# A fused delta-rule attention and maxout FFN kernel: loads asked for in another order, and two blocks written from another queue

## The chip, the cores and the metric

The kernel runs on one core of a Trainium2 chip. A core has TensorE (PE), VectorE (DVE), ScalarE (ACT), GpSimd (POOL) and SyncE (SP), each with its own in-order stream of instructions, and 16 DMA engines[...]. The metric is the device time of one execution in microseconds (us), lower is better; the median of three runs before the change is 530.83 us (530.11 to 531.15).

## The reference

Two stages follow each other. The first is a delta-rule recurrence for 4 batches x 8 heads, 768 steps and head size 48; the second a maxout FFN over the 3072 tokens of width 384.

```python
k_n = k / (norm(k) + 1e-06)
for t in range(S):
    y[:, :, t] = q_t @ state
    v_old = state^T k_t
    state = state + beta_t * outer(k_t, v_t - v_old)
x = y.transpose(0, 2, 1, 3).reshape(B * S, H * D)      # 3072 x 384
h = maximum(maximum(x @ w1, x @ w2), x @ w3)           # 384 -> 768
out = h @ w_out                                        # 768 -> 384
```

## The kernel before, in words

The recurrence is done in 12 chunks (c) of 64 steps. A chunk has two units, n = 2c and 2c + 1, each of two batches with all heads; four units make a group m of two chunks, so there are 6 groups, and group m's tokens are the 512 that FFN stage m takes. For a unit, `turn` (L361, L367) transposes the keys (part 0) and queries (part 1) on PE and copies them to SBUF; `gram` (L438) multiplies keys with keys (`at`, copied at L455) and keys with queries (`pt`, copied at L449 or masked at L422). Within a chunk a triangular system has to be solved. Its 32-wide blocks are gathered as one system per partition: the `at` blocks of a group go to DRAM (`to_dram`, L468, four DMAs a unit), `blocks` reads them back as `x_bl` (L515), and `solve` eliminates on DVE (L551, then pairs of L565 and L569). The result y goes to DRAM (`y_d`, L591) and comes back as `ut` (L600, eight DMAs). Group 0, the opening, does it without DRAM: `to_blocks`, a transpose, the elimination in halves of 16, a transpose back (L573), copies into `ut` (L584 on ACT, L586 on DVE or GpSimd). Then the parts are joined: `halves_z` (p_e, L674) and `halves_u` (p_f, L691; negated copies L681 on DVE, L683 on ACT) for the halves of 16; `join_z` (p_z, L709; copies L712, L714) and `join_u` (p_j, L723; L681, L683) for those of 32. `new` (p_u, L768), `step` (p_s), `to_y` (p_y) and `to_x` (p_x) carry the recurrence and lay the result out as the FFN's input `xt`.

The FFN's weights come as 24 pieces of 384 KB: `fetch` (L215) loads one into `w_bits` (five buffers, oldest first), and one step of `conv` (the generator `weights`) converts one on ACT (L238, L239, L240, into `mant` and `up`, two buffers each) and then joins the piece before it: a shift on DVE (L250) and an add on GpSimd (L254). Pieces 0 to 17 are w1, w2 and w3, 18 to 23 are w_out.

Every engine executes in the order in which the program is written (a manual schedule), so the text is the schedule. After the opening, the loop over `ffn(0)` has 31 steps i, 18 of a half-width p_h (L926), 9 of a full-width one, then the output layer (p_o, L958). In each step the tables name what else is put in: `fetch` and `conv` by i, `FIRST` and `EARLY_LINKS` by letters (t = turn, g = gram, z and j = joins, u = new, s = step, S = a step of `solve`). In EARLY_LINKS the units of g0 to g3 are 8 to 11, at steps 12, 14, 16 and 17. Steps of `solve(1)` lie in steps 0 to 13; its write to DRAM falls in step 12, the reads in step 13. `blocks(2)` reads at step 18. In step 18 `some(conv, 1)` stands ahead of d0 d1 z0 z1, and in step 19 it stands ahead of j0.

Two buffers matter in the opening: unit n's queries lie in place n mod 3 of `qall`, so unit 3's load waits until unit 0's have been turned; and `wo_sb` lends its room to the squares of the keys and to the second system, which is cleared there (L1022) before `solve(1)` starts.

The lines around the first edit (before):

```python
first_blocks()
some(solving, 1)
nc.gpsimd.memset(in_wo(1), 0.0)
load_beta()
load_q(2, (nc.gpsimd, nc.gpsimd))
```

Of the kernel before, what the change touches and what calls it, by code (L numbers as in the profile page):

```python
# [23 lines left out]
def kernel(  # L24
# [31 lines left out]
    nc = tc.nc  # L56
# [50 lines left out]
    one_queue = (nc.sync, nc.sync)  # L107
# [19 lines left out]
    def place(n):  # L127
        return n % NK if n < 12 else n % 4
# [4 lines left out]
    def load_q(n, queues=one_queue):  # L133
        load(q, qpad[n % NQ], n, queues)
# [14 lines left out]
    def load_beta():  # L149
        for i in range(4):  # L150
            cc, half = divmod(i, 2)
            nc.gpsimd.dma_start(
                out=beta_bl[32 * i : 32 * (i + 1)],
                in_=beta.rearrange(
                    "b h (m c f i) -> c f (b h) m i", c=2, f=2, i=BL
                )[cc, half],
            )
# [53 lines left out]
    def fetch(queue=nc.scalar):  # L211
        if fetched[0] < len(pieces):
            _, src, (a, b) = pieces[fetched[0]]
            st = work.tile([128, 2 * 384], U32, name="w_bits", bufs=5)
            queue.dma_start(  # L215
                out=st.rearrange("p (a b) -> p a b", a=a), in_=src
            )
            staged.append(st)
            fetched[0] += 1
# [50 lines left out]
    def small(name, *shape):  # L270
        one = name[-1] == "0" or name[-2:] == "bl" or name == "warm"
        return work.tile([128, *shape], FP32, name=name, bufs=2 - one)
# [60 lines left out]
    def first_norms():  # L333
        norm(nrm_0, ksum_0, small("root0", 2, 2, H), small("newton0", 2, 2, H))
# [10 lines left out]
    def turn(n, parts=(0, 1), copy=nc.scalar.copy):  # L345

        if n not in kqts:
            if n == 6:
                kqts[n] = work.tile([128, KT, TOK], FP32, name="xt").rearrange(
                    "p k t -> p (k t)"  # L350
                )[:, 0 : NP * 4 * C].rearrange(
                    "p (j b i t) -> p j b i t", b=2, i=2, t=C
                )
            else:
                kqts[n] = work.tile([128, NP, 2, 2, C], FP32, name="kqt", bufs=6)
        kqt = kqts[n]
        p_t = ps_two("p_t")
        for i in parts:
            src = (kpad[place(n)], qpad[n % NQ])[i]
            for j in range(NP):  # L360
                nc.tensor.transpose(  # L361
                    p_t[:, i, j * 128 : (j + 1) * 128],
                    src[:, 2 * j : 2 * j + 2],
                    ident,
                )
        some = slice(parts[0], parts[-1] + 1)
        copy(  # L367
            kqt.rearrange("p j b i t -> p i (j b) t")[:, some],
            p_t.rearrange("p i (x t) -> p i x t", t=C)[:, some],
        )  # L370
# [56 lines left out]
    def gram(n, parts=(0, 1), queues=one_queue, copy=nc.scalar.copy, later=False):  # L427
        kqt, g = kqts[n], n % 2
        p_g = ps_two("p_g")

        whole = len(parts) == 2 and not g
        for j in range(NP):
            for par in range(2):
                for bb in range(2):
                    kq = kqt[dims(par), j, bb ^ g]
                    for i in (0,) if whole else parts:
                        c0 = j * 128 + i * C
                        nc.tensor.matmul(  # L438
                            p_g[
                                rows(bb ^ (g * i)), par, c0 : c0 + C * (1 + whole)  # L440
                            ],
                            kq[:, 0],
                            kq if whole else kq[:, i],
                        )
        p_v = p_g.rearrange("p two (j i t) -> p two j i t", j=NP, i=2)
        if 1 in parts:
            pt = pts[n] = square("pt")
            if later:
                copy(by_par(pt), p_v[:, :, :, 1])  # L449
            else:  # L450
                masked(pt, p_v[:, :, :, 1])
        if 0 not in parts:
            return
        at = ats[n] = square("at")
        copy(by_par(at), p_v[:, :, :, 0])  # L455
        if queues:
            to_dram(n, queues)
# [23 lines left out]
    def in_wo(i):  # L481
        n = BL * BL + BL
        return wo_sb.rearrange("p t d -> p (t d)")[:, n * i : n * (i + 1)].rearrange(
            "p (s r) -> p s r", s=2
        )
# [15 lines left out]
    def first_blocks():  # L501
        xs[0] = work.tile([128, 2, HB * BL + HB], FP32, name="x_bl", bufs=1)
        nc.vector.transpose(
            out=in_rows(xs[0]), in_=in_rows(in_wo(0)).rearrange("p x i -> p i x")
        )
# [159 lines left out]
    def halves_z(c):  # L665
        if c > 1:
            halves_t(c)
        at = [ats[2 * c + g] for g in range(2)]
        second = ut[c % NU].rearrange("p g h (f two x) -> p g h f two x", two=2, x=HB)
        for hs, p_v, copy in heads_of(c, "p_e", BL):  # L670
            for i, h in enumerate(hs):
                for bb, g in TILES:
                    r = rows(bb)
                    nc.tensor.matmul(  # L674
                        p_v[rows(bb ^ g), g, i], at[g][r, h], second[r, g, h, :, 1]
                    )
            copy(zs[c % NU][:, :, span(hs)], p_v)
# [294 lines left out]
    def some(gen, n):  # L972
        for _ in range(n):
            if next(gen, gen) is gen:
                break
# [15 lines left out]
    def keys(n, queues=one_queue, copy=nc.scalar.copy):  # L991
        gram(n, (0,), queues, copy)
# [25 lines left out]
    to_blocks(2, (nc.scalar, nc.gpsimd, nc.scalar, nc.gpsimd))  # L1018
    to_blocks(3, (nc.vector, nc.scalar, nc.vector, nc.scalar))
    first_blocks()  # L1020
    some(solving, 1)
    nc.gpsimd.memset(in_wo(1), 0.0)  # L1022
    load_beta()
    load_q(2, (nc.gpsimd, nc.gpsimd))
    p_n = flipped(kflip_0)
    nc.scalar.copy(ksum_0[:, :, 1], p_n.rearrange("p (c h) -> p c h", c=2))
    turn(4, (0,))
# [3 lines left out]
    turn(6, (0,))  # L1031
    turn(0, (1,))
    load_q(3, (nc.gpsimd, nc.gpsimd))
    keys(6)
    gram(0, (1,), None, later=True)
    turn(7, (0,))
# [4 lines left out]
        fetch(nc.sync)  # L1041
    blocks(1)
    load_v(1)
    for n in (2, 3):
        turn(n, (1,))
    for n in (2, 3):
        gram(n, (1,), None, later=True)
    some(solving, HB + 1)
    halves_t(0)
    halves_z(0)  # L1050
    first_norms()
    for c in range(2):
        scale(c, nrm_0[:, c])
# [52 lines left out]
        e=halves_z, f=halves_u, d=turn_t1,  # L1106
    )
    MADE = dict(V=load_v, P=prep_values)
    UNIT = dict(t=turn, g=gram, K=load_k, L=lambda n: load_blocks(n, nc.sync))
    OF_KEYS = dict(S=lambda n: some(solving, n), T=lambda n: turn(n, (1,)), P=lambda n: gram(n, (1,)))  # L1110

    def links(m, names):
        for name in names.split():
# [3 lines left out]
            elif f in MADE and m + 1 < GROUPS:  # L1117
                MADE[f](2 * (m + 1) + i)
            elif f in UNIT and m + 1 < GROUPS:
                UNIT[f](4 * (m + 1) + i)  # L1120
            elif f == "N" and m + 2 < GROUPS:
# [12 lines left out]


    CONVERTED = {*range(6), *range(11, 25)}
    for i, _ in enumerate(ffn(0)):
        if i - 1 in CONVERTED:
            fetch(nc.sync if i < 10 else nc.gpsimd)
        if i in (18, 19, 25):  # L1140
            some(conv, 1)
        if i == 20:
            solving = solve(2)
            some(solving, 1)
        if i == 21:
            some(solving, 3)
        queries(FIRST.get(i, ""))
        links(1, EARLY_LINKS.get(i, ""))
        if i in CONVERTED and i not in (18, 19):
            some(conv, 1)  # L1150
        if 3 < i < 14:
            some(solving, (2, 1, 2, 2, 3, 3, 3, 3, 2, 2)[i - 4])
        if i in (5, 7):
            prep_values(i // 2)
        if i in (1, 7):
            for n in range(2):
                load_k(8 + 2 * (i > 1) + n, (nc.gpsimd, nc.gpsimd))
        if i == 0:
            load_v(3)
        if i in (0, 2):  # L1160
            load_q(5 + i // 2)
        if i == 11:
            load_q(11, (nc.gpsimd, nc.gpsimd))
        if i in (10, 21):
            load_v(4 + i // 21)
        if i == 18:
            blocks(2)
        if i == 23:
            prep_values(4)
        if i > 21:  # L1170
            some(solving, (3, 2, 3, 2, 2, 5, 5, 5, 4)[i - 22])
        if i in (27, 28, 29):
            load_blocks(i - 15, nc.sync)
        if i in (15, 17, 19, 22, 25, 27):
            less_first((15, 17, 19, 22, 25, 27).index(i))
        if 27 <= i < 30:
            turn_first((2 * (i - 27), 2 * (i - 27) + 1))


    RECURS.update(x=y_blocks, w=read_y, X=turn_y, p=prep_values)  # L1180
    UNIT.update(t=turn_blocks, K=lambda n: load_k(n, (nc.gpsimd, nc.gpsimd)))
    MADE.update(V=lambda c: load_v(c, nc.gpsimd))
# [43 lines left out]
```

## Time and profile before

| | before |
|---|---|
| time, median of 3 | 530.83 us |
| profiled span | 528.4 us |
| PE busy | 499.5 us, 95% of the span |
| DVE, ACT, POOL busy | 309.2, 164.7, 186.1 us |
| chain that ended last, by engine | PE 77%, DVE 11%, DMA 4%, SP queue 4% |
| PE waiting for the queries (p_t from qall) | 3.3 us, once |
| PE waiting for ut from y_d (p_z) | 3.0 us, twice |

A busy time is summed over one engine's instructions. The chain is followed back from the last instruction to what released each; its shares say where the time went, while a busy share only says how full an engine was. The first 118 us are where PE isn't full.

### The profile page before, as it was taken

The numbers are of one execution on the slowest core, as the hardware profiler recorded it, in microseconds if no ns is written. First come the engines' busy times: TensorE is split into PE (matmuls) and PEld (weight loads), VectorE is DVE, ScalarE is ACT, GpSimd is POOL, SyncE is SP. The second block draws the span as 40 slices with busy tenths as digits, with TensorE's granted clock in tenths as the row PEclk, the third lists the DMA queues.
The fourth block names the chain that finished last, engine by engine and source line by source line (L and its number), as shares of the span: only waits on it lengthen the run. The fifth ranks groups of instructions, "written<-read, shape, count | busy, mean of one in ns | idle before, by whom it ended". The sixth has DMA issues, their size and how long they took to land.

```text
span 528.4 us, 18036 instructions
## 1 busy us (share of the span) xinstructions
PE 499.5 (95%) x7840; PEld 308.4 (58%) x7840; DVE 309.2 (59%) x695; ACT 164.7 (31%) x302; POOL 186.1 (35%) x306
## 2 busy tenths in 40 slices
PE   6567899979999999999999999999999999999996
PEld 5456677855556555566555565555565555654453
DVE  5855999866997351499662899654887231111100
ACT  5556573685422152120142201242101411011000
POOL 7504255553365471962095880501230000000000
PEclk9855789998999999999999999999999999999999
DMA  8972948494116771654494553734334202130011
GB/s 113 214 157 79 179 124 150 105 261 114 33 37 165 150 145 31 141 131 103 104 165 92 145 138 95 162 54 89 88 85 107 43 2 62 52 68 0 0 27 34
DMA packets 110591, 53.47 MB, mean 101 GB/s; under 512 B 93808, under 2 KB 104976, under 8 KB 110512
## 3 DMA queue, kind: packets, MB, share of 16 engines
q1 hardware_dynamic: 100016, 34.70, 31.4%
q0 software_dynamic: 8384, 17.22, 13.7%
q8 instruction: 62, 1.02, 0.8%
q10 hardware_dynamic: 2112, 0.39, 0.5%
q14 instruction: 17, 0.14, 0.1%
HBM read 39.17 MB, written 13.11 MB: 99 GB/s over the span
## 4 chain that ended last, share of the span: by engine, by line
PE 77%; DVE 11%; DMA 4%; SPq 4%; issue 2%; ACT 1%; POOL 1%; DVEq 0%; ACTq 0%; POOLq 0%
PE p_h L926 33%; PE p_o L958 25%; PE p_g L438 3%; DVE wo_sb L569 3%; PE p_u L768 2%; PE p_m L906 2%; PE p_y L810 2%; SPq L120 2%; DVE tmp L565 2%; PE p_k L740 2%; DMA qall<-in_q_dram 2%; PE p_s L791 1%; PE p_q L740 1%; PE p_j L723 1%; DMA ut<-y_d 1%
## 5 line engine op out<-in xcount | busy, mean ns | idle before, releaser
L926 PE MATMUL p_h<-xt,w_sb 128*128 128x512 f32 (+1 forms) x522 | 221.4, 569 | 2.7 <-DVE h L940 1.3
L926 PEld LDWEIGHTS p_h<-xt,w_sb 128*128 128x128 f32 x522 | 96.8, 194 | 88.8 <-issue 80.5
L958 PE MATMUL p_o<-wo_sb,h 128*128 128x384 f32 x288 | 97.8, 489 | 0.0
L940 DVE TENSOR_TENSOR h<-h,p_h 128x512 f32<-128x512 f32 (+1 forms) x48 | 29.7, 619 | 95.2 <-PE p_h L926 95.1
L958 PEld LDWEIGHTS p_o<-wo_sb,h 128*128 128x128 f32 x288 | 53.7, 190 | 35.7 <-issue 0.5
L565 DVE TENSOR_TENSOR tmp<-x_bl,y_bl 128x31 f32<-128x31 f32 (+20 forms) x139 | 54.0, 388 | 4.1
L964 ACT COPY o_sb<-p_o 128x384 f32<-128x384 f32 x24 | 11.5, 480 | 134.1 <-PE p_o L958 128.1
L569 DVE TENSOR_TENSOR y_bl<-y_bl,tmp 128x31 f32<-128x31 f32 (+20 forms) x139 | 48.5, 349 | 4.8
L936 ACT ACTIVATE h<-p_h 128x512 f32<-128x512 f32 x30 | 17.9, 597 | 87.9 <-PE p_h L926 86.5
L958 PE MATMUL p_o<-w_sb,xt 128*128 128x384 f32 x120 | 42.0, 486 | 0.0
L396 POOL DMA_DIRECT2D turned<-in_q_dram x72 | 39.3, 553 | 5.2 <-POOL turned L391 2.5
L438 PE MATMUL p_g<-kqt 48*64 48x64 f32 (+1 forms) x1216 | 27.5, 240 | 6.0 <-DVE nt_bl L263 3.7
L254 POOL TENSOR_TENSOR w_sb<-mant,up 128x384 int32<-128x384 int32 x18 | 18.6, 1036 | 41.1 <-DVE mant L250 23.5
L438 PEld LDWEIGHTS p_g<-kqt 48*64 48x64 f32 x1216 | 24.2, 141 | 14.4 <-ACT kqt L367 7.3
L958 PEld LDWEIGHTS p_o<-w_sb,xt 128*128 128x128 f32 x120 | 22.8, 190 | 15.9
L120 POOL DMA_DIRECT2D kpad<-in_k_dram x32 | 21.9, 691 | 14.3 <-PE p_s L791 14.3
L287 POOL TENSOR_TENSOR v_t<-v_t,nrm 128x768 f32<-128x768 f32 x12 | 18.2, 1520 | 23.4 <-DVE nrm L266 14.4
L798 DVE TENSOR_TENSOR st<-st,p_s 48x768 f32<-48x768 f32 (+1 forms) x18 | 17.1, 949 | 15.0 <-PE p_s L791 14.8
L422 DVE TENSOR_TENSOR pt<-p_g,mask 128x512 f32<-128x512 f32 x20 | 13.7, 689 | 17.2 <-PE p_g L438 17.2
L139 POOL DMA_DIRECT2D v_t<-in_v_dram x12 | 9.9, 832 | 34.2 <-PE p_u L768 33.3
L391 POOL MEMSET turned<- 128x96 f32 x18 | 3.3, 191 | 50.0 <-DVE kqt L412 50.0
L768 PEld LDWEIGHTS p_u<-v_t,ut 64*64 64x64 f32 x768 | 13.5, 141 | 8.7 <-issue 7.8
(152 smaller groups left out, 618.6 us busy)
## 6 DMA issues: line engine op xcount, KB each, us to landing
w_bits<-in_moe_w_dram SPq DMA_DIRECT2D x14, 384.0 KB, 3.5
out_dram<-o_sb SPq DMA_DIRECT2D x48, 96.0 KB, 2.2
turned<-in_q_dram POOLq DMA_DIRECT2D x72, 48.0 KB, 2.8
kpad<-in_k_dram POOLq DMA_DIRECT2D x32, 96.0 KB, 4.3
y_x<-y SPq DMA_DIRECT2D x16, 192.0 KB
qall<-y_x SPq DMA_DIRECT2D x32, 96.0 KB, 2.7
at_d<-at SPq DMA_DIRECT2D x80, 32.0 KB, 2.4
ut<-y_d SPq DMA_DIRECT2D x40, 64.0 KB, 3.1
```

The source lines that it names most:

```text
L120: queues[bb].dma_start(out=dst[rows(bb ^ g), :, 0:D], in_=src[2 * bb + g, :, c * C : (c + 1) * C, :].rearrange("h p d -> p h d"),)
L254: nc.gpsimd.tensor_tensor(out=dst.bitcast(I32), in0=mant_v.bitcast(I32), in1=up_v, op=ALU.add)
L287: nc.gpsimd.tensor_tensor(out=vts[c], in0=vts[c], in1=nrm[:, :, :, None].to_broadcast([128, 2, H, D]), op=ALU.mult,)
L396: (queue, nc.gpsimd)[i].dma_start(out=t[p0 : p0 + 32, bb, at : at + NP * 2 * D].rearrange("p (j x) -> p j x", j=NP), in_=(k, q)[i][2 * bb ...
L438: nc.tensor.matmul(p_g[rows(bb ^ (g * i)), par, c0 : c0 + C * (1 + whole)], kq[:, 0], kq if whole else kq[:, i],)
L565: nc.vector.tensor_tensor(out=t_v, in0=row.to_broadcast(t_v.shape), in1=column.to_broadcast(t_v.shape), op=ALU.mult,)
L569: nc.vector.tensor_tensor(out=rest, in0=rest, in1=t_v, op=ALU.subtract)
L768: nc.tensor.matmul(p_v[rows(bb ^ g), g, i], ut[c % NU][rows(bb), g, h], rhs[rows(bb), g, h],)
L926: nc.tensor.matmul(p_h, w_sb[i][:, t, f * 128 : (f + 1) * 128], xt[:, t, lo : lo + w], start=(t == 0), stop=(t == KT - 1),)
L936: nc.scalar.activation(out=h, in_=p_h, func=mybir.ActivationFunctionType.Relu)
L940: nc.vector.tensor_tensor(out=h, in0=h, in1=p_h, op=ALU.max)
L958: nc.tensor.matmul(p_o, stays, moves, start=(n == 0), stop=(n == len(terms) - 1))
```

## The change

Three things are changed, all in the order of instructions or in the queue that issues a transfer; the arithmetic stays as it is.

1. In the opening, the load of unit 2's queries is issued by GpSimd ahead of its share of the solve; the clear of the second system and the beta loads go behind the load of unit 3's queries. Unit 2's Gram with its queries follows its turn at once, and unit 3's is put behind `halves_z(0)`, so that the copies into `ut` don't stand behind it.
2. The weight loads of steps 12 to 21 are laid out anew: one in step 8, none in steps 15 to 17, in which the substitution's result is on its way to DRAM and back, and two each in steps 18 and 19. The conversion of step 19 moves behind that step's links.
3. The `at` blocks of units 10 and 11 are written to DRAM through GpSimd's queue instead of SP's.

```diff
     first_blocks()
+    load_q(2, (nc.gpsimd, nc.gpsimd))
     some(solving, 1)
-    nc.gpsimd.memset(in_wo(1), 0.0)
-    load_beta()
-    load_q(2, (nc.gpsimd, nc.gpsimd))
...
     load_q(3, (nc.gpsimd, nc.gpsimd))
+    nc.gpsimd.memset(in_wo(1), 0.0)
+    load_beta()
...
-    for n in (2, 3):
-        turn(n, (1,))
-    for n in (2, 3):
-        gram(n, (1,), None, later=True)
+    turn(2, (1,))
+    gram(2, (1,), None, later=True)
+    turn(3, (1,))
     some(solving, HB + 1)
     halves_t(0)
     halves_z(0)
+    gram(3, (1,), None, later=True)
     first_norms()
...
-    UNIT = dict(t=turn, g=gram, K=load_k, L=lambda n: load_blocks(n, nc.sync))
+    UNIT = dict(
+        t=turn, K=load_k, L=lambda n: load_blocks(n, nc.sync),
+        g=lambda n: gram(n, queues=(nc.gpsimd,) * 2 if n in (10, 11) else one_queue),
+    )
...
     CONVERTED = {*range(6), *range(11, 25)}
+    FETCHED = {8: 1, 12: 1, 13: 1, 14: 1, 18: 2, 19: 2, 20: 1, 21: 1}
     for i, _ in enumerate(ffn(0)):
-        if i - 1 in CONVERTED:
-            fetch(nc.sync if i < 10 else nc.gpsimd)
-        if i in (18, 19, 25):
+        if 0 < i < 7:
+            fetch(nc.sync)
+        for _ in range(FETCHED.get(i, 0)):
+            fetch(nc.gpsimd)
+        if i in (18, 25):
             some(conv, 1)
...
-        if i in CONVERTED and i not in (18, 19):
+        if i in CONVERTED and i != 18:
             some(conv, 1)
```

## The prediction

> **What bounds the kernel now.** I read the page's slices first. PE is full from about the tenth slice on (one slice is 13.2 us); what can be won lies ahead of that and in the dip of the granted clock in the tenth digit.
>
> ```profile
> PE   6567899979999999999999999999999999999996
> PEclk9855789998999999999999999999999999999999
> ```
>
> Then the chain that ended last, in order of time (start us, us, what). It shows the two places that the change touches.
>
> ```profile
> 22.19 5.67 DMA qall<-in_q_dram
> 28.00 2.03 PE p_t L361 x8
> 30.02 1.97 PE p_g L438 x63
> ...
> 32.02 0.59 ACT pt L449
> ...
> 32.62 1.05 ACT ut L584
> ...
> 102.95 6.06 DMA y_d<-wo_sb
> ...
> 112.07 4.78 DMA ut<-y_d
> ...
> 116.98 0.96 PE p_z L709 x51
> 117.93 4.47 PE p_h L926 x6
> ```
>
> First place: the queries of units 2 and 3 arrive at 27.9, PE turns them, makes two Grams, ACT copies them out, and only then does ACT copy the solved block (ut, L584). DVE's timeline shows that the block had been ready earlier, and who waited for ACT:
>
> ```profile
> 27.10 1.92 DVE L573 STREAM_TRANSPOSE x_bl<-y_bl 128x1024 f32<-128x1024 f32 x1
> 34.78 0.71 DVE L646 STREAM_TRANSPOSE t<-ut 128x512 f32<-128x512 f32 x1 [4.49 <-ACT ut L584]
> ```
>
> The transpose ends at 29.02; ACT starts at 32.62: 3.6 us lost on the chain. From 54 to 100 us the chain is DVE's (the elimination L565/L569 and what is put between), with hardly a wait, so an earlier start there is kept.
>
> Second place: the result of the substitution goes to DRAM (6.06 us for the second 256 KB) and comes back; PE stands at p_z for 0.39 and 2.65 us, and the next p_h takes 4.47 us where its neighbours take 2.77, because the clock fell: 119.5 to 122.9 us at half. GpSimd's timeline shows what ran on the DMA engines and on GpSimd then (brackets: idle before, and releaser):
>
> ```profile
> 101.43 0.75 POOL L215 DMA_DIRECT2D w_bits<-in_moe_w_dram  x1
> 102.20 1.01 POOL L254 TENSOR_TENSOR w_sb<-mant,up 128x384 int32<-128x384 int32 x1
> 103.15 0.77 POOL L215 DMA_DIRECT2D w_bits<-in_moe_w_dram  x1
> ...
> 105.32 0.75 POOL L215 DMA_DIRECT2D w_bits<-in_moe_w_dram  x1
> ...
> 107.34 0.57 POOL L215 DMA_DIRECT2D w_bits<-in_moe_w_out_dram  x1
> 108.87 1.00 POOL L254 TENSOR_TENSOR w_sb<-mant,up 128x384 int32<-128x384 int32 x1 [0.96 <-ACT up L240]
> ```
>
> After 123 us PE has no long idle left, so what is won before it should stay to the end.
>
> **What the skill says.** "TensorE: Matmul & The Clock Gate", What's actually happening: the array runs at half clock after an idle window of about 3.4 us and comes back after a busy one. The trace agrees: one 3.4 us stretch at half after the p_z waits. "DMA: Bandwidth & Descriptors", Queues, rings and completion order: each DMA engine takes turns between the queues that have work. The trace agrees: between 105 and 110 us the DMA share is 0.97, and the y_d write takes 6.06 us where the same 256 KB take 4.1 at the median of the later stages. "SBUF — State Buffer", Who interferes with whom: GpSimd's writing of descriptors can be held up while DVE has the shared ports. Here GpSimd's ten issues at L215 lie between 0.55 and 0.78 us beside a busy DVE, so I do not expect it to matter.
>
> **The change part by part.**
>
> *Queries sooner.* Unit 2's load now goes out when GpSimd is free of the block copies, at 12.5 instead of 21.5; the clear of y_bl behind it ends near 15 and is needed by L542 at 17.72: hidden. Unit 3's load needs PE's turn of unit 0's queries (ends 19.0), so it goes out near 19.1 instead of 22.9. With the 4 to 5.7 us to landing of these loads both are there by 18 and by 25. The clear of wo_sb and the beta loads move behind them, to about 24; the next elimination wants them at 57: nothing. Then PE turns unit 2 at 24.7 at once, makes its Gram, turns unit 3 by 27.4, and ACT has copied all by about 28.1, before 29.02. So ACT copies ut from 29.05: 3.57 us sooner.
>
> *Gram 3 moved behind halves_z(0).* It is no longer ahead of ut, but it now stands between p_e and p_f. At half clock its 32 records take 1.0 us (64 took 1.99). ACT, which is in order, waits for it after z: before, sqrt (L261) started at 36.31 and the first L683 at 38.12, 1.81 us later. In the old time frame the new Gram ends at 37.45, its copy takes to 38.05, and L683 starts at 39.9, 1.8 us later than before. DVE's first L681 stood at 38.58 because of the norm, so from there on the delay is 1.6. Net: 3.57 - 1.6 = 2.0. The masked pt of 1.50 us at 42.78 (others take 0.69) collides with GpSimd, whose scaling now comes 0.6 us earlier against it; I allow 0.2. **Opening: 2.2 us.**
>
> *No weight load at steps 15 to 17.* Ten loads remain: one at step 8 (GpSimd free at 87.2, a buffer free since step 5), 12, 13, 14, then two at 18 and 19. Loads 13 and 14 wait now for a buffer from ACT's conversions, until about 102 and 104.3. So beside the y_d write, whose packets run from 105 to 109 in the trace's packet records, only the rest of load 13 and load 14 are left. 128 packets of 4 KB at 0.16 us on 16 engines are 1.3 us; with those two about 2.2. I take the write's end at 107.3 instead of 109.0, eight read issues at 0.5 us each from 106.3 to 110.4 (at 179.84 eight took 4.08), and 2.1 us to the last landing as at 413.53: 112.5. PE wants the two halves at 113.1 and 113.95 in this frame (p_h, L926, ends at 113.09). No wait, and so no dip of the clock.
>
> *Grams 10 and 11 written by GpSimd.* Eight issues of 32 KB leave SP. The trace has none of this kind on GpSimd; bounds are 0.49 us (the 2 KB beta) and 0.83 (192 KB of v); I take 0.61 for 256 pieces of 128 B, 2.45 us for four. Behind them in GpSimd's order stands the same step's joining of a weight piece (L254), and for that waits ACT: mant and up have two buffers, so the conversion two steps on needs the join. GpSimd: four issues 109.3 to 111.75 (ACT's copy ends 109.2), join to 112.75 (before: 109.87), four issues to 115.2, join to 116.2 (before: 112.67). ACT's conversion of step 18 stands ahead of the z copies: it starts at 116.25, takes 1.4 (114.84 to 116.24 before), and the two z copies of the first half take 1.2 (116.24 to 117.40): PE can start p_j at 119.0. PE has p_z twice (1.7) and p_h (2.77) from 113.09, so it is at p_j at 117.6 and waits 1.4 us. Before, p_j started at 122.33. **Second place: 122.33 - 119.0 = 3.3 us.**
>
> *Conversion of step 19 behind the links; two loads at once.* Piece 18 is asked for at 116.2 and lands 4.4 us later at the row's median, near 121; ACT wants it at 121.4 after L683. The blocks read (x_bl, 3.3 us) follows GpSimd's last write and lands near 122 to 123; ACT's root stands ahead of the second L683 then, and PE wants the result at p_s only at about 127. Both hidden, with 1 to 2 us to spare.
>
> Sum: 2.2 + 3.3 = 5.5 us; 530.8 - 5.5 = **525.3 us**.
>
> **The rivals.**
>
> A. *Both waits go whole.* The issues on GpSimd are short or the conversions don't wait: p_j at 117.6, so 4.7 us, and the opening's full 3.6: 530.8 - 8.3 = 522.5; with only one of the two about 524. For: ACT is idle for a good part around 113 to 122. Against: the order in which ACT stands behind GpSimd is plain in the code, and L238 is released by L254 in the waits of this window.
>
> B. *The wait returns.* The read back still comes late, or the joins and conversions eat the rest; only the opening is left: 530.8 - 2.2 = 528.6. For: the write still meets loads 13 and 14, and its first packets come 2.1 us after issue[...]. Against: the 1.5 MB of loads beside write and read are gone.
>
> C. *Nothing to measure*: opening lost by a late query or by the Gram between p_e and p_f, second place half: 530 to 531.
>
> D. *Slower.* GpSimd's issues take 1.5 us each because DVE holds it up: four are 6 us, the second join ends near 123.3, ACT's conversion starts there, z ends at 126, PE starts p_j 3.7 us later than before, and a second dip of 1.7 may follow (4.47 - 2.77); less 2.2 of the opening: 534.0. For: no such issue is in the trace. Against: the mean of no kind of issue there is over 0.83 us.
>
> **How the numbers follow.** My forecast 0.46, A (or one of its halves) 0.18, B 0.19, C 0.06, D 0.11. The range 522.6 to 529.8 holds the forecast, B and nearly all of A; D and most of C stay outside. Faster by over 0.2% (under 529.8) is forecast, A and B: 0.83; same 0.05; slower 0.12.
>
> **What would show it.** Right: ACT's L584 starts near 29; DVE's idle before L646 falls from 4.49 to about 1; L683 of p_f starts near 36.3; no idle before p_z and no half clock near 120; p_h of step 19 takes 2.8 us; a new wait of 1 to 1.5 us at p_j, ended by ACT's z, with POOL L254 ahead of L238. Wrong: unit 3's queries landing after 27.5 (the opening falls); PE idle at p_z still over 1 us (B); no PE idle at p_j (A); GpSimd's L468 issues over 1 us each (D); ACT waiting for w_bits or x_bl with PE idle behind it after 121, a step I count as hidden.

## The result and the profile after

The changed kernel takes 524.6 us (median of 4; 524.22 to 525.86) beside 530.99 us for the kernel before in the same runs: a ratio of 0.9886, with a 95% interval of 0.9865 to 0.9907. That is 6 us; 5.5 were forecast, a time of 525.3 us. A later set of runs gave 0.9884 (0.9848 to 0.9921). One run of the experiments, of 531.69 us in e5, was in a slower state and stands in no ratio.

The page's slices after (13.1 us each): PE is as full as before, but the digit 8 in the tenth slice of the clock is a 9.

```profile
PE   6667898989999999999999999999999999999996
PEclk9855899999999999999999999999999999999999
```

The opening. ACT's timeline after (start us, us, engine, line, operation, tiles and shapes, count, and in brackets the idle time before and what ended it): the copies into ut start 0.03 us after the transpose L573 ends at 29.15, and unit 3's Gram is copied only then, behind z.

```profile
28.43 0.59 ACT L367 COPY kqt<-p_t 128x512 f32<-128x512 f32 x1 [0.89 <-PE p_t L361]
29.18 2.12 ACT L584 COPY ut<-x_bl 32x512 f32<-32x512 f32 x2 [0.17 <-DVE x_bl L573]
32.47 0.37 ACT L677 COPY z<-p_e 128x256 f32<-128x256 f32 x1 [1.17 <-PE p_e L674]
34.23 0.59 ACT L449 COPY pt<-p_g 128x512 f32<-128x512 f32 x1 [1.39 <-PE p_g L438]
...
36.36 0.24 ACT L683 ACTIVATE ut<-p_f 16x128 f32<-16x128 f32 x1
```

DVE's idle time before L646 is 0.95 us where it was 4.49.

The second place. PE's timeline after: p_z runs through (128 records in 1.61 us) with no wait, the p_h behind it takes 2.84 us, and there is a new wait at p_j, 1.36 and 0.36 us, both ended by ACT's z.

```profile
107.66 2.84 PE L926 MATMUL p_h<-xt,w_sb 128*128 128x512 f32 x6
110.43 1.61 PE L709 MATMUL p_z<-ut,at 32*32 32x32 f32 x128
111.97 2.84 PE L926 MATMUL p_h<-xt,w_sb 128*128 128x512 f32 x6
116.17 0.24 PE L723 MATMUL p_j<-z,t 32*32 32x32 f32 x2 [1.36 <-ACT z L712]
116.78 0.74 PE L723 MATMUL p_j<-z,t 32*32 32x32 f32 x62 [0.36 <-ACT z L714]
```

The chain that ended last passes there from GpSimd's issues to its joins, to ACT's conversion, to z, to PE (start us, us, what):

```profile
110.77 1.64 POOL at_d L468 x3
...
112.49 0.58 POOL at_d L468
...
113.08 1.02 POOL w_sb L254
...
114.12 0.56 ACT mant L238
114.69 0.52 ACT up L239
115.21 0.49 ACT up L240
115.70 0.42 ACT z L712
```

One table for the profiles (without that of e5) shows where the time came from. Up to the end of the transpose L573 DVE does the same work in all of them and waits for nothing that was changed. The first three columns count from it; the last is the distance from `solve(1)`'s first product (L551) to p_s of step 21, across the DRAM round trip. What each experiment changed is told below.

| profile of | L584 | first L683 | L551 | L551 to p_s |
|---|---|---|---|---|
| before | 3.60 | 9.10 | 30.80 | 71.05 |
| after | 0.03 | 7.21 | 28.38 | 67.81 |
| opening alone (e1) | 1.55 | 8.73 | 29.87 | 71.28 |
| loads and writes alone (e2) | 3.48 | 8.97 | 30.45 | 68.11 |
| Grams on SP (e3) | 1.61 | 8.78 | 29.92 | 70.68 |
| Grams on SP, second profile (e11) | 0.03 | 7.22 | 28.64 | 70.37 |
| loads as before (e4) | 0.04 | 7.21 | 27.71 | 71.61 |
| Gram 3 ahead of the solve (e7) | 1.93 | 7.42 | 29.03 | 70.66 |
| after, again (e8) | 0.04 | 7.21 | 27.66 | 68.81 |
| conversion later (e10) | 1.53 | 8.71 | 29.86 | 66.65 |
| Gram 3 late (e6) | 0.03 | 5.52 | 27.56 | 67.79 |
| both moves (e9) | 0.04 | 5.53 | 26.30 | 66.35 |
| both moves, again (e12) | 0.03 | 5.52 | 28.94 | 67.75 |

From before to after the opening gave 30.80 - 28.38 = 2.4 us and the second place 71.05 - 67.81 = 3.2 us; 2.2 and 3.3 were forecast. One pair of profiles does not settle the first: the seven with the changed kernel's opening (after, e1, e3, e4, e8, e10, e11) have L551 at 27.66 to 29.92, 28.9 on average, the two with the old one at 30.80 and 30.45. That is 1.8 us, and the pair lies above it. At p_s the changed kernel is 5.5 us ahead and at its end 5.9: of the rest, 0.3 us is a p_z at 414.69 that takes 1.72 us before and 1.44 after.

### The profile page after: what moved, and what is told of

It reads as the page before. It is cut to its first block, busy times and chain, and to the rows that moved or that the text cites. A ratio compares the mean times of both kernels' runs of the same rounds, so it can differ in the third digit from the quotient of the medians.

```text
span 522.5 us, 18030 instructions
## 1 busy us (share of the span) xinstructions
PE 495.1 (95%) x7840; PEld 305.9 (59%) x7840; DVE 311.0 (60%) x695; ACT 164.4 (31%) x302; POOL 190.6 (36%) x314
## 4 chain that ended last, share of the span: by engine, by line
PE 79%; DVE 12%; ACT 2%; DMA 2%; issue 1%; POOL 1%; SPq 1%; DVEq 0%; ACTq 0%; POOLq 0%
PE p_h L926 34%; PE p_o L958 26%; PE p_g L438 3%; DVE tmp L565 3%; PE p_m L906 2%; PE p_u L768 2%; PE p_y L810 2%; DVE wo_sb L569 2%; DMA kmore<-in_k_dram 2%; PE p_k L740 2%; PE p_j L723 2%; PE p_s L791 1%; PE p_q L740 1%; SPq L120 1%; PE p_z L709 1%
## 5 line engine op out<-in xcount | busy, mean ns | idle before, releaser
L926 PE MATMUL p_h<-xt,w_sb 128*128 128x512 f32 (+1 forms) x522 | 218.9, 564 | 2.8 <-DVE h L940 1.3
L565 DVE TENSOR_TENSOR tmp<-x_bl,y_bl 128x31 f32<-128x31 f32 (+20 forms) x139 | 51.7, 372 | 4.1
L438 PE MATMUL p_g<-kqt 48*64 48x64 f32 (+1 forms) x1216 | 27.5, 239 | 6.8 <-DVE nt_bl L263 3.8
L254 POOL TENSOR_TENSOR w_sb<-mant,up 128x384 int32<-128x384 int32 x18 | 18.3, 1018 | 24.3 <-DVE mant L250 21.7
```

The lines of the kernel that those rows point to most:

```text
L254: nc.gpsimd.tensor_tensor(out=dst.bitcast(I32), in0=mant_v.bitcast(I32), in1=up_v, op=ALU.add)
L438: nc.tensor.matmul(p_g[rows(bb ^ (g * i)), par, c0 : c0 + C * (1 + whole)], kq[:, 0], kq if whole else kq[:, i],)
L565: nc.vector.tensor_tensor(out=t_v, in0=row.to_broadcast(t_v.shape), in1=column.to_broadcast(t_v.shape), op=ALU.mult,)
L926: nc.tensor.matmul(p_h, w_sb[i][:, t, f * 128 : (f + 1) * 128], xt[:, t, lo : lo + w], start=(t == 0), stop=(t == KT - 1),)
```

## The experiments

The runs of a set share the runs of the kernel before; the sets ran on several chips, and within that of e1 to e4 the kernel before lies between 528.4 and 537.6 us, so ratios are given with their intervals and mechanisms are read from the traces.

**The opening alone (e1)**: the three opening edits on the kernel before, all else as it was.

> Only the opening's edits on the kernel before. Theory (two separate gains that add up): 2.2 to 2.6 us under before, so 528.4 to 528.8 us; ACT's L584 starts near 29, p_x some 2.3 us earlier; the PE wait at p_z (3 us) and the 3.4 us at half clock near 117 to 120 stay as they were. Rival (the earlier start is eaten at the DRAM round trip, because the transfers there do not come sooner): within 0.6 us of before, the PE wait at p_z grown to 5 us or more.

529.84 us, 0.9969 of before (0.9951 to 0.9987). p_z still waits, 0.29 and 2.40 us, and the clock falls there. So the gain is kept across the round trip (71.28 in the table beside 71.05), and the rival falls. The size is under the theory: 1.6 us at the ratio (0.7 to 2.6), 0.9 in this profile's L551. PE was at half clock for 6.8 us from 15.7 on and again from 25.9, in the profile after for 3.4 from 16.4 and again from 26.6, so the turns and Grams of the queries ended 1.5 us later and ACT came to ut late (1.55 in the table).

**Loads and writes alone (e2)**: the changed kernel with the opening's lines as before.

> Only the new order of weight loads, the later conversion of step 19 and the two Gram blocks on GpSimd, with the opening as before. Theory: 2.8 to 3.5 us under before, 527.5 to 528.2 us; no PE wait at p_z, no half clock near 120, a new PE wait of 1.4 to 1.9 us at p_j. Rival (the wait at p_z went only because the opening's shift changed what the transfers meet): PE still waits over 1 us at p_z and the time is 529.5 us or more.

527.82 us, 0.9923 (0.9894 to 0.9951), some 4 us, and 2.9 us in the table's last column. The time is the theory's, the profile only in part: there is no half clock near 120, but PE waits 1.03 us at p_z, and since it comes later to p_j, 0.36 us is all that is seen of the new wait there. With e1 the two parts make 0.31% + 0.77% = 1.08%, and the whole change 1.14%: they add up.

**Gram blocks on SP (e3, e11)**:

```diff
-        g=lambda n: gram(n, queues=(nc.gpsimd,) * 2 if n in (10, 11) else one_queue),
+        g=gram,
```

> The changed kernel with the two Gram blocks written from SP's queue as before; the new loads and the opening stay. Theory (the eight issues on GpSimd hold up the joins, these ACT's conversions, these the z copies, and that is the 1.7 us wait at p_j): the wait at p_j falls under 0.5 us; the blocks read goes out at about 118.5 instead of 115.1 and lands near 122, which stays hidden; 1.0 to 1.7 us faster than the changed kernel, near 523.2 us. Rival (the writes on GpSimd are needed: from SP the blocks read lands so late that ACT's root holds up the joins' copies and PE): the wait at p_j goes, but a wait of 1 us or more comes after 120; 524.5 to 527 us.

528.45 us, 0.9939 (0.9907 to 0.9971): about 3 us slower than the changed kernel, whose interval, up to 0.9907, this one only touches. My theory had half of it: the wait at p_j is gone, and a larger one came, 5.06 us at p_s. Then a second profile of the same kernel:

> The kernel with the two Gram blocks on SP's queue, for a second profile. If what was seen in the first is its mechanism: no PE idle at p_j, the read of x_bl lands after 124, and PE waits 2 to 5 us at p_s for ACT's u, which stands behind the root of x_bl. If the first profile was a chance: the read lands near 122 and PE waits under 0.5 us at p_s.

528.79 us, and the same picture. PE's timeline of this second profile, then its chain, then GpSimd's loads of weights:

```profile
128.31 1.96 PE L791 MATMUL p_s<-u,kmore 64*64 64x48 f32 x64 [4.71 <-ACT u L773]
```

```profile
111.08 6.05 DMA at_d<-at
117.14 3.39 DMA at_d<-at
120.56 5.38 DMA x_bl<-at_d
125.96 0.03 ACT root_bl L261
...
127.45 0.81 ACT u L773
```

```profile
110.41 1.12 POOL L215 DMA_DIRECT2D w_bits<-in_moe_w_out_dram  x2
...
112.49 1.09 POOL L215 DMA_DIRECT2D w_bits<-in_moe_w_out_dram  x2
```

SP's twelve writes take from 109.6 to 117.4 to issue: by the chain the last goes out only when the one of 111.08 has landed, 6.05 us after its issue, and it lands 3.39 us later. In the changed kernel the last write goes out at 112.49 and lands after 2.55. So the blocks are read at 120.56 instead of 115.14, the read takes 5.4 us, ACT stands 7.3 us at the root, and PE 4.7 at p_s. The writes on GpSimd cost 1.7 us at p_j and save this. The kernel before had SP's writes too, but there PE stood at p_z and at half clock meanwhile, which hid them: ACT's wait for x_bl was 1.4 us and ended at 125.71, before PE came to the second p_j at 125.79.

Which property of the edit saves it is not settled. Freed of the eight issues, GpSimd asks for the four weight loads of steps 18 and 19 at 110.41 to 113.04, beside SP's writes; in the changed kernel they go out at 114.02 to 116.64, when the writes are issued. SP's full queue and these early loads were changed together, and no run has the one without the other.

**Loads as before (e4)**: the two conditions on `fetch` and `conv` put back, the rest of the change kept.

> The changed kernel with the weight loads and the conversion of step 19 where they were before; the Gram blocks stay on GpSimd and the opening stays. Theory (the loads beside the write and the read make them late): the y_d write takes about 6 us again, PE waits 2 to 3 us at p_z and the clock dips; 527.5 to 529.5 us. Rival (freeing SP's queue of eight issues was what removed the wait): no PE wait over 1 us at p_z, under 526 us.

529.35 us, 0.996 (0.9943 to 0.9977). PE's timeline: the wait at p_z is back in three pieces, 3.2 us in all, and the half clock with it (6.8 us from 113.4; the p_h behind it takes 4.67 us in the chain).

```profile
111.29 0.90 PE L709 MATMUL p_z<-ut,at 32*32 32x32 f32 x60 [0.40 <-DMA ut<-y_d]
113.73 0.31 PE L709 MATMUL p_z<-ut,at 32*32 32x32 f32 x4 [1.50 <-DMA ut<-y_d]
115.36 1.07 PE L709 MATMUL p_z<-ut,at 32*32 32x32 f32 x60 [1.31 <-DMA ut<-y_d]
```

The y_d write takes 5.93 us on the chain. The loads made the round trip late; freeing SP's queue of eight writes does not by itself remove the wait, and the ratio is close to that of the opening alone (0.9969).

**Conversion of step 18 behind the z copies (e5, e10)**:

```diff
-        if i in (18, 25):
+        if i == 25:
             some(conv, 1)
...
-        if i in CONVERTED and i != 18:
+        if i in CONVERTED:
             some(conv, 1)
```

> The changed kernel with the conversion of step 18 behind that step's links instead of ahead of them, so that ACT makes the z copies before it waits for GpSimd's join. Theory (that wait of ACT is the whole cause of PE's 1.7 us at p_j): no PE idle over 0.3 us at p_j; the z copies start near 113 instead of 115.6; 1.5 to 2.0 us faster than the changed kernel, about 0.985 of before. Rival (ACT only pays it one place later: the conversion then stands ahead of the copies of p_j, and PE waits at p_u or p_s): within 0.5 us of the changed kernel.

524.82 us, 0.9845 (0.981 to 0.988): 2 us under e8 by the ratios, but the intervals overlap. The profile read here is that of another run:

> The kernel with the conversion of step 18 behind the z copies, for an undisturbed profile of it. Theory: no PE idle over 0.3 us at p_j; z copies right behind the copy of h; near 524.5 us. Rival: PE waits at p_u or p_s instead, with ACT's root (x_bl) or the conversion ahead of the copies it wants.

525.29 us. No wait at p_j is left: ACT goes from h to z at once, as expected. But ACT's timeline shows a part of the gain taken at the next step:

```profile
113.81 0.58 ACT L934 COPY h<-p_h 128x512 f32<-128x512 f32 x1
114.27 0.56 ACT L712 COPY z<-p_z 32x512 f32<-32x512 f32 x1
...
123.40 0.26 ACT L261 ACTIVATE root_bl<-x_bl 128x32 f32<-128x32 f32 x1 [2.34 <-DMA x_bl<-at_d]
```

PE waits 0.53 us at p_s behind that. The distance to p_s is 66.65 where it is 67.81 after: 1.2 of the expected 1.5 to 2.0 us.

**Unit 3's Gram elsewhere (e6, e7)**: behind `to_x(0)`, and back ahead of the solve.

```diff
     halves_z(0)
-    gram(3, (1,), None, later=True)
...
     to_x(0)
+    gram(3, (1,), None, later=True)
```

> The changed kernel with unit 3's Gram moved from behind halves_z(0) to behind to_x(0), where PE waits for the copies anyway. Theory (between p_e and p_f it costs 1.6 to 1.8 us, because ACT stands in order behind it): the first L683 of p_f starts near 34.7 instead of 36.36; p_x 1.3 to 1.7 us earlier; 1.2 to 1.7 us faster than the changed kernel. Rival (the conversion on ACT or the p_f matmuls hold the same step, so the place of the Gram is free): L683 within 0.4 us of 36.4 and the time within 0.5 us.

525.26 us, 0.9859 (0.9825 to 0.9893): 1.3 us under e8, with overlapping intervals. The first L683 comes 7.21 - 5.52 = 1.7 us sooner, as the theory had it, but L551 only 0.8 sooner than in the profile after, and 0.1 sooner than in e8's. GpSimd's timeline names what takes the rest: it waits for the values of the second chunk, and behind it in order stand the copies into ut and the join that ACT's next conversion waits for.

```profile
42.28 1.47 POOL L287 TENSOR_TENSOR v_t<-v_t,nrm 128x768 f32<-128x768 f32 x1 [5.42 <-DMA v_t<-in_v_dram]
43.70 2.21 POOL L586 COPY ut<-x_bl 32x512 f32<-32x512 f32 x2
46.30 0.99 POOL L254 TENSOR_TENSOR w_sb<-mant,up 128x384 int32<-128x384 int32 x1 [0.39 <-DVE mant L250]
```

In the three profiles with the late Gram this scaling starts at 41.73 (e9), 42.28 (e6) and 43.28 (e12), and the copy that begins the FFN's input (xt, L877) at 49.38, 49.73 and 50.96: 7.5 to 7.7 us later each time, where it is 8.6 in the profile after. In these three the landing of v has become what the opening waits for.

In e7 the diff is the line put behind `turn(3, (1,))` instead.

> The changed kernel with unit 3's Gram back ahead of the solve's last steps, behind its turn, so that of the opening's edits only the earlier loads and the order of unit 2's Gram are left. Theory (with the queries there early the Gram costs about as much ahead of ut as behind halves_z): L584 starts at 30.5 to 31 instead of 29.2, nothing stands between p_e and p_f, p_x and the time within 0.6 us of the changed kernel. Rival (the move of the Gram is what won the opening): 1.5 to 2.3 us slower than the changed kernel.

526.4 us, 0.9886 (0.9848 to 0.9924), the changed kernel's own ratio. ut starts 1.9 us later and the first L683 only 0.2 later. So the place that the change gave this Gram won nothing that can be measured, and what the opening won came from the earlier loads with unit 2's Gram behind its turn. The times alone do not exclude the rival: each interval is some 2 us wide to either side. The second place, whose code is that of the changed kernel, came off badly in this profile (70.66): PE waits 0.26 and 0.92 us at p_z, and the p_h behind it takes 4.54 us.

**The changed kernel beside them (e8)**:

> The changed kernel itself, beside the others on the same chip: 0.986 to 0.991 of before. It is the measure for the three beside it.

525.79 us, 0.9884 (0.9848 to 0.9921). In this profile of the same kernel PE waits 1.16 and 0.22 us at p_z, and the clock falls, for 3.4 us from 113.8. The round trip is not safely hidden, it is just about in time:

```profile
112.95 0.25 PE L709 MATMUL p_z<-ut,at 32*32 32x32 f32 x4 [1.16 <-DMA ut<-y_d]
113.42 0.83 PE L709 MATMUL p_z<-ut,at 32*32 32x32 f32 x60 [0.22 <-DMA ut<-y_d]
114.18 4.35 PE L926 MATMUL p_h<-xt,w_sb 128*128 128x512 f32 x6
```

**Both moves (e9, e12)**: the diffs of e5 and e6 together.

> The changed kernel with both moves: the conversion of step 18 behind the z copies, and unit 3's Gram behind to_x(0). Theory (the two costs are separate): their gains add, 1.5 to 3 us faster than the changed kernel, 0.980 to 0.985 of before. Rival (the earlier start only meets the read of the blocks, x_bl, which then holds up ACT's root and with it PE at p_s): no better than the better of the two alone, 0.985 to 0.987, with a PE wait of 1 us or more at p_s.

523.32 us, 0.9875 (0.9836 to 0.9915).

> The kernel with both moves once more, because the interval of its first run overlaps that of the changed kernel. If the moves' gains are real: 0.981 to 0.987 of before, a median near 523 to 524 us, the upper end of the interval under 0.99. If the first was a chance: 0.988 or more, a median of 525.5 us or more.

524.11 us, 0.9859 (0.9823 to 0.9895). The first profile is the shortest of all, a span of 520.0 us, with no wait at p_z or p_j and 0.22 us at p_s; the second has 0.90 us at p_z and 1.01 at p_s, and its v landed 1.5 us later. By the ratios the two are 0.5 and 1.3 us under the changed kernel in e8, and no better than each move alone (0.9845 and 0.9859). All these intervals overlap: that this version is the faster one is not settled, and a sum of the two gains is not seen. The rival's wait at p_s is there in e12.

## Why the prediction was right

**Opening, 2.2 us.** 2.4 in the one pair of profiles, 1.8 over all of them, 1.6 (0.7 to 2.6) timed alone: the size is somewhat too large, and that the pair came so near it is partly luck. Its steps held: L584 forecast at 29.05 and seen at 29.18; the first L683 at 36.3 by the forecast and at 36.36. Three terms were off. The queries of unit 3 were to be there by 25; PE waited 0.40 us for them until 27.31, since the two issues began at 19.85, not 19.1, and the loads landed 5.95 and 6.65 us after issue where 5.7 was the longest that I had allowed. That it cost nothing is luck too: the limit was 27.5, and in e6 and e7 the turn began at 27.75 and 27.57. The 0.2 us for a masked pt did not come: one still takes 1.36 us. And the Gram's 1.6 us between p_e and p_f was right (1.7 in e6), but taking it out is not worth that much, since another wait, for v, stands behind it.

**No load in steps 15 to 17.** The effect was right and e4 shows the cause. The margin was too generous: I had the last of the read land 0.6 to 1.4 us ahead of PE. SP's reads began at 104.40, which in the frame of before (2.6 us later here) is the 106.99 of before, not 106.3, and took 5.09 us to issue, not 4.1. So the start of the read gained nothing; what was won is its issue, 5.09 us instead of 6.64, and its landing. That left no margin. With the loads as before PE waits 2.7 to 3.2 us at p_z (before, e1, e4); with the new ones it waits not at all in after, e3, e9 and e11, 0.2 us in e6 and e10, and 0.9 to 1.4 us in e2, e7, e8 and e12.

**The clock.** In the profile after the dip went with the wait: p_h took 2.84 us instead of 4.47 to 4.54. (The dip of before lies at 118.8 to 122.2 us by the trace, not at 119.5 to 122.9.) The Trainium skill, "TensorE: Matmul & The Clock Gate" (What's actually happening), has this half rate after an idle window of about 3.4 us. The traces have it after less: PE's longest idle time ahead of the dip is 2.65 us in before, 1.16 in e8 and 0.92 in e7. Nor does the length of the wait decide it, since the new 1.7 us at p_j in after and the 1.03 us at p_z in e2 brought no dip.

**Grams on GpSimd.** The new wait at p_j was forecast at 1.4 us and is 1.7, by the path that was named: four issues of 0.58 us (0.61 taken), join, conversion, z. In e10 only ACT's conversion was moved, in e3 and e11 only the writes, and each time the wait is gone: that shows the path. What the prediction lacked is the other side: it counted this edit as a cost only. e3 and e11 show that without it PE waits 5.1 and 4.7 us at p_s, and e4 shows that it alone does not keep p_z from waiting. The sum came out right with this edit's role wrong: by the working as it stands, leaving the edit out would have been the faster kernel.

**Conversion of step 19 and paired loads.** Hidden, as said, in the profile after: ACT's L683, L238 and root follow each other at 117.95, 119.17 and 120.61 with no wait for w_bits or x_bl. Elsewhere ACT does wait for x_bl, 0.53 us in e8 and 2.34 in e10, and in e10 PE waits behind it.

**The rivals.** A (both waits whole) is refuted by the wait at p_j, C by the time, D by issues of 0.58 us. B, the wait that returns, is refuted by the time and in the profile after, but its sign, over 1 us at p_z, is there in e8's profile of the same kernel: a part of B is true in some executions.

## What to carry to other kernels

When a wait goes, ask what it had been hiding: here a late read of the next system was free only while PE stood at p_z, and the edit that looked like pure cost paid for that. When an engine is freed of issues, ask what it will issue earlier instead: here four weight loads moved up beside the writes. Price an issue by what stands behind it in its engine's order and by the two-deep buffer that this stage hands on, not by its own 0.6 us. And where an early start is won in front of a load that comes at its own time, look for that load's landing before counting the whole. And take a second profile of the same kernel before a margin of less than 1 us is called hidden.

## What was not expected of the hardware

The same kind of write, 32 KB in pieces of 128 B, landed 2.1 to 3.4 us after issue from GpSimd's queue in the changed kernel, and 2.8 to 4.2 us in e4, with weight loads nearer to it. Of the sixteen on SP in e11 the trace gives few landings, 3.88 and 5.67 us, and by the chain 6.05 and 3.39; one of the twelve last issues took 1.44 us, the others 0.5 or less. The Trainium skill, "Trainium Kernel Development and Optimization", Key Constraints, has it that issuing from several engines "only saves the sequencer's issue time". The traces agree in the main: where e11 reads the blocks 5.4 us later, the last write is issued 4.65 us later and takes 0.84 us longer to land. But that issue itself waited for a landing, and the weight loads around the writes moved too, so what of it is the queue stays open.

The stretches at half clock do not lie at one place of the program. Each that lies whole in a profile lasts 3.41 us or a multiple of it, up to 34.13, and the opening's first one begins at 16.40 and 18.27 in the two profiles of the changed kernel (after and e8) and at 15.66 and 15.18 in e1 and e10, whose code is the same up to there. Where it ends at 22.0 to 24.0 (e1, e3, e10) ut starts 1.5 to 1.6 us late; where it ends at 19.8 to 21.7 (after, e4, e8, e11) ut starts on time, in e11 too, where it lasts 6.8 us. A part of the scatter between runs of one kernel may come from there; how much, no run shows.
